# Decay rows kept in SBUF and copied per head into two fixed operand tiles, in a decay attention with two feed-forward layers

## The chip, the cores and the metric

One core of one Trainium2 chip runs the whole program in one launch. The metric is device time in microseconds (us): the median of three runs, and for one execution that was profiled, its own time and the span of its instructions. Engines are called as in the profile: PE is TensorE (matmuls), PEld its weight loads, DVE is VectorE, ACT ScalarE, POOL GpSimd, SP SyncE, which here issues nearly all DMAs in the order of the program.

## What is computed

```
scores = scale * q @ k.T                          # 4 x 8 heads, 576 x 576, head size 64
log_f  = log(clip(f, 1e-4, 1)); cum = cumsum(log_f)
scores = where(causal, -1e9, scores + cum[i] - cum[j])
attn   = softmax(scores);  out = attn @ v
x = out as (2304, 512)
x = (h * relu6(h + 3) / 6) @ w_out,   h = x @ w_in       # 512 -> 2048 -> 512
x = (max(h, 0) + alpha * min(h, 0)) @ w_out2, h = x @ w_in2
```

## The kernel before

The program has two stages: attention, about the first 210 us, and the two feed-forward layers. Attention goes over 16 pairs of heads. A pair is nine units: four blocks of 128 query rows of the even head (positions 0 to 3), one unit that holds the last 64 rows of both heads (position 4, which reads the even head's tiles and then the odd head's, L375 and L377), and four blocks of the odd head (positions 5 to 8). A loop over units writes each engine's work by hand: scores of unit t, maxima of unit t-1, exponentials of t-2, transposes and evictions of t-5; the weights of the feed-forward layers are converted in between by a table of unit numbers (`CONV_ATT`).

The scores of one head take two matmuls that add up in PSUM. Line L363 multiplies `k1` and `q1` (128 rows). Line L364 multiplies `k2` and `q2` (68 rows): rows 0 to 63 hold the low part of q and the high part of k, and rows 64 to 67 carry the decay: the two words of `cum` (high and low) against rows of 1 and of -1. The four tiles of a head come from a pool with three buffers of each.

Where the decay rows come from: in the prologue `cum` of all heads is made in one SBUF tile of 64 partitions, and from it and some constants two DRAM tensors `aq_d` and `ak_d` are written (L502, L504, L523 to L528). For the first two heads `aug_rows` copies the rows from SBUF straight into the tiles (L495 to L498). For each later head h, `prep_head` (at position 3 for the next pair's even head, 7 for its odd head) issues two DMAs that read the four rows of `q2` and of `k2` from DRAM:

```
nc.sync.dma_start(out=q2[64:68].bitcast(F32), in_=aq_d[h % 2, h // 2])
nc.sync.dma_start(out=k2[64:68].bitcast(F32), in_=ak_d[h % 2, h // 2])
```

Then POOL writes `q1` and `k1` (L93). Two units later `prep_low` makes the low parts (POOL L331, DVE L332), and `copy_k` copies the high part of k from `k1` into `k2` by a DMA from SBUF to SBUF (L325; for heads 2 and 3 POOL does it within `prep_head`). `load_head` (L295) reads q and k of a head from DRAM into one of three `rqk` buffers.

SP issues DMAs strictly in this written order, and a DMA that has to wait holds all behind it. In the trace SP issues the copies of a head well ahead of the unit in which they stand, since their buffers are free early.

Of the kernel before, what the change touches and what calls it, by code (L numbers as in the profile page):

```python
# [8 lines left out]
F32 = mybir.dt.float32  # L9
I64 = mybir.dt.int64  # L10
U32 = mybir.dt.uint32
F32R = mybir.dt.float32r
# [9 lines left out]
def decay_attention_ffn2_kernel(ctx, tc, qk, v, f, wi1, wo1, wi2, wo2, alpha, out):  # L22
    nc = tc.nc
# [15 lines left out]
    KT = 5  # L39
# [41 lines left out]
    wo_d = [[dram.tile([128, 2, FT * DM], F32, name=f"wod{ff}{g}") for g in range(NG)] for ff in range(2)]  # L81

    f_d = [dram.tile([128, 4, KH * 256], F32, name=f"fd{g}") for g in range(NC)]
    aq_d = dram.tile([2, 32, 4, QW], F32, name="aq_d")
    ak_d = dram.tile([2, 32, 4, S], F32, name="ak_d")

    def scaled(engine, dst, src, scale=1.0):
        if engine == "A":
# [189 lines left out]
    def attention():  # L278
        with ExitStack() as ax:
# [9 lines left out]
            ps_pv = ax.enter_context(tc.tile_pool(name="ps_pv", bufs=1, space=PSUM))  # L289

            raws, slots, vs, pts, sm, rcs, rcb = {}, {}, {}, {}, {}, {}, {}

            def load_head(h):
                raw = rawp.tile([128, QW + S], F32, tag="raw", name="rqk")
                nc.sync.dma_start(out=raw, in_=qk[h])  # L295
                raws[h] = (raw[:, 0:QW], raw[:, QW:QW + S])
# [3 lines left out]
                nc.sync.dma_start(out=vs[p], in_=v[p // NPAIR, p % NPAIR])  # L300

            def op_tiles(h):
                slots[h] = (opsp.tile([128, QW], F32R, tag="q1", name="q1"),
                            opsp.tile([68, QW], F32R, tag="q2", name="q2"),
                            opsp.tile([128, S], F32R, tag="k1", name="k1"),
                            opsp.tile([68, S], F32R, tag="k2", name="k2"))
                return slots[h]

            def prep_head(h):
                if h not in slots:  # L310
                    q1, q2, k1, k2 = op_tiles(h)
                    nc.sync.dma_start(out=q2[64:68].bitcast(F32), in_=aq_d[h % 2, h // 2])
                    nc.sync.dma_start(out=k2[64:68].bitcast(F32), in_=ak_d[h % 2, h // 2])
                q1, q2, k1, k2 = slots[h]
                rq, rk = raws[h]
                e = AS0[h] if h < 2 else AS
                scaled(e[0], q1, rq, SCALE)
                scaled(e[1], k1, rk)
                if h < 4:
                    scaled(e[2], k2[0:64], rk[0:64])  # L320

            def copy_k(h):
                q1, q2, k1, k2 = slots[h]
                if h >= 4:
                    nc.sync.dma_start(out=k2[0:64].bitcast(F32), in_=k1[0:64].bitcast(F32))  # L325

            def prep_low(h):
                q1, q2, k1, k2 = slots[h]
                rq, rk = raws.pop(h)
                low = nc.vector if h < 2 and LS0[h] == "V" else nc.gpsimd  # L330
                low.tensor_sub(out=k1[64:128], in0=rk[64:128], in1=k1[64:128].bitcast(F32))  # L331
                nc.vector.scalar_tensor_tensor(  # L332
                    out=q2[0:64], in0=rq[0:64], scalar=SCALE, in1=q1[0:64].bitcast(F32),
                    op0=ALU.mult, op1=ALU.subtract)
# [128 lines left out]
                        d.pop(key)  # L463


            NPP = 64
            px = ExitStack()
            pro = px.enter_context(tc.tile_pool(name="pro", bufs=1))
            fl = pro.tile([NPP, S], F32, name="fl")
# [2 lines left out]

            zero = pro.tile([NPP, S], F32, name="zero")
            cum = pro.tile([NPP, S], F32, name="cum")
            aq = pro.tile([NPP, 2, QW], F32, name="aq")
            pro.tile([NPP, 2 * ((KT - 1) * PR + S) - 3 * S - 2 * QW], F32, name="room")
            ak = pro.tile([NPP, 4, S], F32R, name="ak")
            hl = ak[:, 2:4, :]
            nc.gpsimd.memset(zero, 0.0)
            nc.gpsimd.memset(aq, -1.0)  # L480
            for a in range(2):
                nc.gpsimd.memset(aq[32 * a:32 * a + 32, :, 576 - 64 * a:640 - 64 * a], 0.0)

            def aug_consts(a):
                o0 = 576 - 64 * a
                q1, q2, k1, k2 = op_tiles(a)
                (nc.gpsimd if a else nc.vector).memset(k2[64:68].bitcast(F32), 1.0)
                nc.vector.memset(q2[64:68].bitcast(F32), -1.0)
                nc.vector.memset(q2[64:68, o0:o0 + 64].bitcast(F32), 0.0)

            def aug_rows(a):
                r, t0 = slice(32 * a, 32 * a + 1), 512 + 64 * a
                q1, q2, k1, k2 = slots[a]
                w = S if a == 0 else 512
                nc.sync.dma_start(out=q2[64:66, 0:w].bitcast(F32), in_=hl[r, :, 0:w].bitcast(F32))  # L495
                (nc.sync if a else nc.scalar).dma_start(out=k2[66:68].bitcast(F32), in_=hl[r].bitcast(F32))
                if w < S:
                    nc.sync.dma_start(out=q2[64:66, t0:t0 + TAIL].bitcast(F32), in_=hl[r, :, 512:S].bitcast(F32))  # L498

            load_head(1)  # L500
            nc.sync.dma_start(out=alpha_sb, in_=alpha)
            nc.sync.dma_start(out=aq_d.rearrange("a h r c -> (a h) r c")[:, 2:4], in_=aq)  # L502
            for a in range(2):
                nc.sync.dma_start(out=aq_d[a, :, 0:2, 576 - 64 * a:640 - 64 * a],  # L504
                                  in_=zero[32 * a:32 * a + 32, 0:128].rearrange("p (r c) -> p r c", r=2))
            aug_consts(0)
            aug_consts(1)
            make_identity(nc, identb)
            nc.gpsimd.memset(maskb, 0.0)
            nc.gpsimd.affine_select(out=maskb, in_=maskb, pattern=[[-1, 128]], compare_op=ALU.is_ge,  # L510
                                    fill=-1.0e9, base=0, channel_multiplier=1)
            nc.gpsimd.memset(ak[:, 0:2, :].bitcast(F32), 1.0)
            nc.vector.tensor_scalar(out=fl, in0=fl, scalar1=1e-4, scalar2=1.0, op0=ALU.max, op1=ALU.min)
            nc.scalar.activation(out=fl, in_=fl, func=AF.Ln)
            nc.vector.tensor_tensor_scan(out=cum, data0=fl, data1=zero, initial=0.0, op0=ALU.add, op1=ALU.add)
# [2 lines left out]
            nc.vector.tensor_sub(out=hl[:, 1, :], in0=cum, in1=hl[:, 0, :].bitcast(F32))  # L518
            aug_rows(0)
            prep_low(0)  # L520
            aug_rows(1)
            load_head(2)
            nc.sync.dma_start(out=aq_d.rearrange("a h r c -> (a h) r c")[:, 0:2, 0:512], in_=hl[:, :, 0:512].bitcast(F32))  # L523
            for a in range(2):
                ps, t0 = slice(32 * a, 32 * a + 32), 512 + 64 * a
                nc.sync.dma_start(out=aq_d[a, :, 0:2, t0:t0 + TAIL], in_=hl[ps, :, 512:S].bitcast(F32))
            for a in range(2):
                nc.sync.dma_start(out=ak_d[a, 0:NP], in_=ak[32 * a:32 * a + NP].bitcast(F32))  # L528
            load_head(3)
            nc.gpsimd.memset(three, 3.0)  # L530
            make_identity(nc, ident)
# [37 lines left out]
            for t in range(len(units) + max(LV, PB) + 1):  # L569
                now = todo.pop(t, [])  # L570
                for ch in ORD:
                    if ch == "D":
                        for fn in now:
                            fn()
                    if ch == "S" and t < len(units):
                        live[t] = stage1(units[t])
                    for c, lag, fn in (("M", LM, maxes), ("E", LE, exps)):
                        if ch == c and 0 <= t - lag < len(units):
                            live[t - lag] = fn(*live[t - lag])
                    for c, lag, fn in (("T", LT, transposes), ("V", LV, evac)):  # L580
                        if ch == c and 0 <= t - lag < len(units):
                            live[t - lag] = fn(units[t - lag], *live[t - lag])
                if t < len(units):
                    p, ab, i = units[t]
                    pos = t % 9
                    if ab == 1 and i == 3:
                        for d, fn in ((RD, lambda p=p: recips(p)), (SD, lambda p=p: spread(p)),
                                      (PA, lambda p=p: stage3(p, 0)), (PB, lambda p=p: stage3(p, 1))):
                            todo.setdefault(t + d, []).append(fn)
                    if pos == 2:  # L590
                        load_v(p)
                    if pos == QA and 2 * p + 2 < 2 * NP:
                        prep_head(2 * p + 2)
                        todo.setdefault(t + QL, []).append(lambda h=2 * p + 2: prep_low(h))
                        todo.setdefault(t + QL, []).append(lambda h=2 * p + 2: copy_k(h))
                        if p:
                            load_head(2 * p + 3)
                    if pos == QB and 2 * p + 3 < 2 * NP:
                        prep_head(2 * p + 3)
                        todo.setdefault(t + QL, []).append(lambda h=2 * p + 3: prep_low(h))  # L600
                        todo.setdefault(t + QL, []).append(lambda h=2 * p + 3: copy_k(h))
                        if 2 * p + 4 < 2 * NP:
                            load_head(2 * p + 4)
                elif t == len(units) + LE:
                    rx.close()
                    ffn_open()
                for fn in side.pop(t, []):
                    fn()
                for _ in range(DRAIN.get(t, 0)):
                    step()  # L610
# [303 lines left out]
```

## Time and profile before

| | |
|---|---|
| median of 3 runs | 981.56 us (980.86 to 982.42) |
| the profiled execution, its own time | 982.49 us |
| its span, first to last instruction | 980.7 us |
| mean granted clock of TensorE | 0.996 of full speed |
| busy share of the span: PE, DVE, POOL, ACT | 97%, 72%, 61%, 55% |
| chain that ended last: PE, DVE, other | 85%, 8%, 7% |

A busy share is the time in which an engine had an instruction under way. PE is busy nearly all the time, so what counts is the few stretches in which it waits, and how long its instructions take. The chain is followed back from the last instruction to what released each step.

### The profile page before, as it was taken

The page shows a single profiled execution, that of the slowest core. Times are in us where ns is not written, and L with a number is a line of the kernel's source. Part 1 is how long each engine was busy: PE and PEld are TensorE (multiplying, and loading weights), DVE is VectorE, ACT ScalarE, POOL GpSimd, SP SyncE. Part 2 cuts the span into 40 slices and gives each one's busy share as a digit, 9 for nine tenths or more (in the row PEclk, how much of TensorE's full clock was granted, in tenths as well). Part 3 has the DMA queues.
Part 4 walks back from the last instruction along what each step waited for, and adds up shares of the span by engine and source line. Part 5 has one row for each costly group of instructions (what it writes and reads, how often), then busy time and mean ns, then how long its engine had stood idle before and what let it go on. Part 6 is the DMA issues. An engine that isn't in the chain of part 4 may idle for free.

```text
span 980.7 us, 15789 instructions
## 1 busy us (share of the span) xinstructions
PE 955.6 (97%) x5488; PEld 860.4 (88%) x5488; DVE 705.7 (72%) x1274; ACT 539.7 (55%) x1348; POOL 594.4 (61%) x583
## 2 busy tenths in 40 slices
PE   5999999999999999999999999999999999999998
PEld 4767766678999999999999999899898988898897
DVE  7898979956697777876788666347897778625454
ACT  5678877777555554555564456644454546343231
POOL 7567589956646665578476379565646668422231
PEclk9999999999999999999999999999999999999999
DMA  7646576501414443410468732413434410253541
GB/s 211 201 136 213 181 250 196 144 35 43 161 65 182 183 183 108 160 59 9 166 246 312 272 130 108 161 65 140 173 118 182 182 65 17 103 204 139 216 161 64
DMA packets 36195, 145.79 MB, mean 149 GB/s; under 512 B 4860, under 2 KB 4860, under 8 KB 33012
## 3 DMA queue, kind: packets, MB, share of 16 engines
q1 hardware_dynamic: 36112, 144.79, 42.0%
q8 instruction: 43, 0.70, 0.3%
q14 instruction: 36, 0.29, 0.1%
q10 hardware_dynamic: 4, 0.00, 0.0%
HBM read 97.21 MB, written 43.42 MB: 143 GB/s over the span
## 4 chain that ended last, share of the span: by engine, by line
PE 85%; DVE 8%; issue 2%; POOL 2%; ACT 1%; SPq 1%; DMA 1%; POOLq 0%; DVEq 0%; ACTq 0%
PE o L744 20%; PE hA L704 20%; PE o L742 19%; PE hC L704 10%; PE hB L704 5%; PE pv L453 4%; DVE nm L340 2%; PE tp L396 2%; PE sc L363 2%; DVE q L332 1%; PE sc L364 1%; DVE pt L407 1%; POOL g L687 1%; DMA k<-ak_d 1%; PE sc L375 0%
## 5 line engine op out<-in xcount | busy, mean ns | idle before, releaser
L687 POOL TENSOR_TENSOR g<-t,g 128x384 fp32r<-128x384 f32 x192 | 205.6, 1071 | 287.6 <-ACT g L686 270.4
L742 PE MATMUL o<-g,wo 128*128 128x384 f32 x1152 | 232.2, 340 | 1.8 <-POOL wo L187 1.1
L704 PE MATMUL hA<-xh,wi 128*128 128x384 f32 x768 | 224.3, 338 | 1.1 <-DVE hD L718 0.7
L744 PE MATMUL o<-wo,g 128*128 128x512 f32 x864 | 223.2, 394 | 0.0
L742 PEld LDWEIGHTS o<-g,wo 128*128 128x128 f32 x1152 | 205.0, 189 | 3.2 <-POOL wo L187 1.4
L686 ACT CAST g<-t 128x384 fp32r<-128x384 f32 x192 | 98.6, 514 | 176.8 <-DVE t L681 91.8
L744 PEld LDWEIGHTS o<-wo,g 128*128 128x128 f32 x864 | 160.6, 188 | 25.8
L762 DVE TENSOR_TENSOR r<-o,r 128x512 f32<-128x512 f32 x126 | 86.7, 688 | 86.2 <-PE o L744 85.7
L704 PEld LDWEIGHTS hA<-xh,wi 128*128 128x128 f32 x768 | 141.5, 188 | 4.7 <-DVE hD L718 1.0
L704 PE MATMUL hA<-xl,wi 128*128 128x384 f32 x384 | 129.5, 337 | 0.0
L751 DVE SCALAR_TENSOR_TENSOR r<-o,r 128x384 f32<-128x384 f32 x168 | 92.1, 552 | 49.1 <-PE o L742 48.3
L704 PE MATMUL hC<-xh,wi 128*128 128x384 f32 x384 | 114.4, 338 | 0.0
L348 ACT ACTIVATE p<-sc,nm 128x128 f32<-128x128 f32 (+4 forms) x160 | 84.2, 530 | 16.6 <-DVE nm L340 14.5
L340 DVE TENSOR_REDUCE nm<-sc 128x1 f32<-128x128 f32 (+4 forms) x160 | 71.6, 469 | 6.1 <-PE sc L365 4.0
L704 PEld LDWEIGHTS hA<-xl,wi 128*128 128x128 f32 x384 | 72.1, 188 | 3.2
L704 PEld LDWEIGHTS hC<-xh,wi 128*128 128x128 f32 x384 | 71.3, 189 | 2.1 <-issue 0.2
L248 POOL TENSOR_TENSOR xl<-r,xh 128x384 fp32r<-128x384 f32 x59 | 69.7, 1197 | 3.3 <-ACT xh L243 2.8
L396 PE MATMUL tp<-ident,p 128*128 128x128 f32 x384 | 68.6, 282 | 1.0 <-ACT pt L412 0.6
L363 PE MATMUL sc<-k,q 128*128 128x256 f32 (+2 forms) x128 | 55.0, 429 | 12.2 <-DVE k L331 8.8
L709 ACT COPY s<-hA 128x384 f32<-128x384 f32 x96 | 45.8, 477 | 35.1 <-PE hA L704 34.9
L704 PE MATMUL hC<-xl,wi 128*128 128x384 f32 x192 | 65.0, 338 | 0.0
L704 PE MATMUL hB<-xh,wi 128*128 128x384 f32 x192 | 57.1, 338 | 0.0
(133 smaller groups left out, 1725.6 us busy)
## 6 DMA issues: line engine op xcount, KB each, us to landing
wid<-wi SPq DMA_DIRECT2D x24, 896.0 KB
wi<-wid SPq DMA_DIRECT2D x12, 1792.0 KB
rqk<-in_qk SPq DMA_DIRECT2D x32, 608.0 KB
raw<-in_wi SPq DMA_DIRECT2D x32, 512.0 KB
raw<-in_wo SPq DMA_DIRECT2D x32, 512.0 KB
wod<-wo SPq DMA_DIRECT2D x24, 512.0 KB
wo<-wod SPq DMA_DIRECT2D x12, 1024.0 KB
vt<-in_v SPq DMA_DIRECT2D x16, 320.0 KB
```

Of the source, the lines that this page charges most:

```text
L248: e.tensor_sub(out=XS[k][1][:, b, c], in0=x, in1=XS[k][0][:, b, c].bitcast(F32))
L340: nc.vector.tensor_reduce(out=nm[:, i:i + 1], in_=src, axis=AX.X, op=ALU.max, negate=True)
L348: nc.scalar.activation(out=pt[:, c0:c0 + cw], in_=src, func=AF.Exp, bias=nm[:, 0:1], scale=1.0, accum_out=dsts[i])
L363: nc.tensor.matmul(out=sc[:, 0:n], lhsT=q1[:, qs], rhs=k1[:, 0:n], start=True, stop=False)
L396: nc.tensor.transpose(tp[:, j, :], pt[:, 128 * j:128 * j + 128], ident)
L686: nc.scalar.copy(out=gt[n][i][:, 0], in_=hold["g"])
L687: nc.gpsimd.tensor_sub(out=gt[n][i][:, 1], in0=hold["g"], in1=gt[n][i][:, 0].bitcast(F32))
L704: nc.tensor.matmul(out=h, lhsT=a, rhs=b[:, x, kc], start=new and kc + e == 0, stop=kc == KH - 1 and e == 2, skip_group_check=not new)
L742: nc.tensor.matmul(out=o[:, 0:NB], lhsT=a[:, cs], rhs=b, start=st, stop=sp)
L744: nc.tensor.matmul(out=o, lhsT=b[:, cs], rhs=a, start=st, stop=sp)
L751: later(0, lambda: nc.vector.scalar_tensor_tensor(out=acc, in0=o[:, 0:NB], scalar=1.0 / 6.0, in1=acc, op0=ALU.mult, op1=ALU.add))
L762: nc.vector.tensor_add(out=acc, in0=o, in1=acc)
```

## The change

The two DRAM tensors and the eight DMAs that fill them go, with the POOL memsets behind them. The tile of `cum` words, now called `hl`, stays in SBUF through the whole attention stage. `q2` and `k2` are no longer taken from the pool of three: there is one fixed pair of tiles for all even heads (`lowq[0]`, `lowk[0]`) and one for all odd heads (`lowq[1]`, `lowk[1]`), so the constant rows are written once. For every head `aug_rows` now copies the two rows of `cum` into `q2` and into `k2` from SBUF: two DMAs for an even head, three for an odd one. These are issued in `copy_k`, which stands two units later than `prep_head` (position 5 for the even head, position 0 of the next pair for the odd head) and now ahead of `prep_low`. For heads 2 and 3 the POOL copy of k's high part moves from `prep_head` to there. In the prologue the loads of heads 2 and 3 stand further ahead.

```diff
-    aq_d = dram.tile([2, 32, 4, QW], F32, name="aq_d")
-    ak_d = dram.tile([2, 32, 4, S], F32, name="ak_d")
...
+            lowq = [lowp.tile([68, QW], F32R, name=f"q2{a}") for a in range(2)]
+            lowk = [lowp.tile([68, S], F32R, name=f"k2{a}") for a in range(2)]
+            hl = lowp.tile([NPP, 2, S], F32R, name="hl")
...
-                slots[h] = (opsp.tile([128, QW], F32R, tag="q1", name="q1"),
-                            opsp.tile([68, QW], F32R, tag="q2", name="q2"),
-                            opsp.tile([128, S], F32R, tag="k1", name="k1"),
-                            opsp.tile([68, S], F32R, tag="k2", name="k2"))
+                slots[h] = (opsp.tile([128, QW], F32R, tag="q1", name="q1"), lowq[h % 2],
+                            opsp.tile([128, S], F32R, tag="k1", name="k1"), lowk[h % 2])
...
             def prep_head(h):
-                if h not in slots:
-                    q1, q2, k1, k2 = op_tiles(h)
-                    nc.sync.dma_start(out=q2[64:68].bitcast(F32), in_=aq_d[h % 2, h // 2])
-                    nc.sync.dma_start(out=k2[64:68].bitcast(F32), in_=ak_d[h % 2, h // 2])
-                q1, q2, k1, k2 = slots[h]
+                q1, q2, k1, k2 = op_tiles(h)
...
-                if h < 4:
+                if h < 2:
                     scaled(e[2], k2[0:64], rk[0:64])
...
             def copy_k(h):
                 q1, q2, k1, k2 = slots[h]
+                aug_rows(h)
                 if h >= 4:
                     nc.sync.dma_start(out=k2[0:64].bitcast(F32), in_=k1[0:64].bitcast(F32))
+                else:
+                    scaled("P", k2[0:64], raws[h][1][0:64])
...
-            def aug_rows(a):
-                r, t0 = slice(32 * a, 32 * a + 1), 512 + 64 * a
-                q1, q2, k1, k2 = slots[a]
+            def aug_rows(h):
+                a = h % 2
+                row, t0 = 32 * a + h // 2, 512 + 64 * a
+                r = slice(row, row + 1)
+                q2, k2 = lowq[a], lowk[a]
                 w = S if a == 0 else 512
                 nc.sync.dma_start(out=q2[64:66, 0:w].bitcast(F32), in_=hl[r, :, 0:w].bitcast(F32))
-                (nc.sync if a else nc.scalar).dma_start(out=k2[66:68].bitcast(F32), in_=hl[r].bitcast(F32))
+                (nc.sync if h else nc.scalar).dma_start(out=k2[66:68].bitcast(F32), in_=hl[r].bitcast(F32))
                 if w < S:
                     nc.sync.dma_start(out=q2[64:66, t0:t0 + TAIL].bitcast(F32), in_=hl[r, :, 512:S].bitcast(F32))
...
             aug_rows(0)
             prep_low(0)
+            load_head(2)
             aug_rows(1)
-            load_head(2)
-            nc.sync.dma_start(out=aq_d.rearrange("a h r c -> (a h) r c")[:, 0:2, 0:512], in_=hl[:, :, 0:512].bitcast(F32))
...
             load_head(3)
...
-                        todo.setdefault(t + QL, []).append(lambda h=2 * p + 3: prep_low(h))
                         todo.setdefault(t + QL, []).append(lambda h=2 * p + 3: copy_k(h))
+                        todo.setdefault(t + QL, []).append(lambda h=2 * p + 3: prep_low(h))
```

How SP's queue changes is seen at two places. The first is the prologue, from the copies of the first heads' decay rows on (`rqk` is the load of a head, `ak` or `hl` the tile of `cum` words). Before:

```order
L495 DMA q2_172<-ak_160 2x1x576
L495 DMA q2_179<-ak_160 2x1x512
L496 DMA k2_181<-ak_160 2x1x576
L498 DMA q2_179<-ak_160 2x1x64
L295 DMA rqk_209<-in_qk 128x1216
L523 DMA aq_d_118<-ak_160 64x2x512
L526 DMA aq_d_118<-ak_160 32x2x64 x2
L528 DMA ak_d_119<-ak_160 16x2304 x2
L295 DMA rqk_216<-in_qk 128x1216
L300 DMA vt_262<-in_v 128x640
L312 DMA q2_273<-aq_d_118 4x640
L313 DMA k2_275<-ak_d_119 4x576
```

and now:

```order
L489 DMA q20_150<-hl_154 2x1x576
L298 DMA rqk_196<-in_qk 128x1216
L489 DMA q21_151<-hl_154 2x1x512
L490 DMA k21_153<-hl_154 2x1x576
L492 DMA q21_151<-hl_154 2x1x64
L298 DMA rqk_201<-in_qk 128x1216
L303 DMA vt_249<-in_v 128x640
L489 DMA q20_150<-hl_154 2x1x576
L490 DMA k20_152<-hl_154 2x1x576
```

The load of head 2 moves ahead of three copies, the writes to DRAM are gone, and head 2's rows come from `hl`.

The second place is the turn from the tenth to the eleventh pair, about 130 us into the span, where the converted weights are stored to DRAM (`wid`); `raw` is a fetch of weights, `vt` of v. Before:

```order
L325 DMA k2_2147<-k1_2146 64x576
L192 DMA wid00_83<-wi_1001 128x1792
L300 DMA vt_2239<-in_v 128x640
L312 DMA q2_2255<-aq_d_118 4x640
L313 DMA k2_2257<-ak_d_119 4x576
L295 DMA rqk_2262<-in_qk 128x1216
L192 DMA wid00_83<-wi_1001 128x1792
L118 DMA raw_2265<-in_wi1 128x512
L325 DMA k2_2257<-k1_2256 64x576
```

and now:

```order
L489 DMA q21_151<-hl_154 2x1x512
L490 DMA k21_153<-hl_154 2x1x576
L492 DMA q21_151<-hl_154 2x1x64
L323 DMA k21_153<-k1_2103 64x576
L190 DMA wid00_83<-wi_976 128x1792
L303 DMA vt_2196<-in_v 128x640
L298 DMA rqk_2215<-in_qk 128x1216
L190 DMA wid00_83<-wi_976 128x1792
L116 DMA raw_2218<-in_wi1 128x512
L489 DMA q20_150<-hl_154 2x1x576
L490 DMA k20_152<-hl_154 2x1x576
L323 DMA k20_152<-k1_2212 64x576
```

The copies of the odd head (21) now write the one pair of odd tiles, and stand with all that follows behind them; the copies of the even head (22) follow the stores as the copy of `k2` did.

## Rows read from the trace of the kernel before

**Rows 1.** The busy time of each engine by stretch, with clock, DMA share, GB/s.

```profile
core 0: us, PE busy (x) PEld busy (x) DVE busy (x) ACT busy (x) POOL busy (x), PEclk, DMA share, GB/s
31.00:55.00 24.00, 23.49 (x183) 16.92 (x182) 21.50 (x44) 18.35 (x67) 12.79 (x13) 1.00 0.56 177
245.00:600.00 355.00, 354.90 (x2019) 354.50 (x2019) 270.92 (x478) 187.42 (x379) 225.57 (x211) 1.00 0.43 156
```

**Rows 2.** The chain that ended last, in order of time, 8 to 80 us.

```profile
17.19 4.98 DMA k<-ak_d
```

**Rows 3.** PE's timeline: start, us, line, idle time before.

```profile
19.24 0.36 PE L363 MATMUL sc<-k,q 128*128 128x256 f32 x1
22.30 0.35 PE L364 MATMUL sc<-k,q 68*128 68x256 f32 x1 [2.70 <-DMA k<-ak_d]
...
27.49 0.29 PE L377 MATMUL sc<-k,q 68*128 68x288 f32 x1
...
35.19 0.28 PE L364 MATMUL sc<-k,q 68*128 68x256 f32 x1
...
38.96 0.30 PE L377 MATMUL sc<-k,q 68*128 68x288 f32 x1
```

**Rows 4.** POOL's timeline, the low part of head 2's k.

```profile
17.51 1.41 POOL L331 TENSOR_TENSOR k<-rqk,k 64x576 fp32r<-64x576 f32 x1
```

**Rows 5.** Stretches after that wait, columns as in rows 1.

```profile
23.90:27.20 3.30, 3.30 (x16) 2.78 (x15) 2.90 (x7) 2.35 (x8) 2.86 (x4) 0.50 0.87 318
27.30:30.60 3.30, 3.30 (x31) 2.65 (x30) 2.97 (x7) 2.38 (x9) 3.13 (x4) 1.00 0.46 97
```

**Rows 6.** PE's timeline: two ends of odd heads, and the units that follow.

```profile
34.21 0.40 PE L364 MATMUL sc<-k,q 68*128 68x512 f32 x1
...
38.43 0.29 PE L377 MATMUL sc<-k,q 68*128 68x288 f32 x1
...
194.16 0.39 PE L364 MATMUL sc<-k,q 68*128 68x512 f32 x1
...
199.02 0.30 PE L377 MATMUL sc<-k,q 68*128 68x288 f32 x1
```

**Rows 7.** SP's timeline: copies within SBUF, start and time of the issue.

```profile
9.96 0.56 SPq L498 DMA_DIRECT2D q<-ak  x1
10.56 0.40 SPq L295 DMA_DIRECT2D rqk<-in_qk  x1
...
112.66 0.47 SPq L325 DMA_DIRECT2D k<-k  x1
```

**Rows 8.** Short stretches after the copy at 112.66, columns as in rows 1.

```profile
114.60:114.80 0.20, 0.20 (x3) 0.03 (x3) 0.20 (x2) 0.20 (x2) 0.20 (x1) 1.00 0.15 46
114.80:115.00 0.20, 0.20 (x4) 0.20 (x4) 0.20 (x3) 0.20 (x1) 0.20 (x1) 1.00 0.00 0
```

**Rows 9.** SP's timeline at the turn to the eleventh pair.

```profile
129.26 0.47 SPq L325 DMA_DIRECT2D k<-k  x1
129.82 0.55 SPq L192 DMA_DIRECT2D wid<-wi  x1
...
136.45 0.47 SPq L325 DMA_DIRECT2D k<-k  x1
```

**Rows 10.** A stretch behind these issues, columns as in rows 1.

```profile
136.00:138.00 2.00, 2.00 (x21) 1.60 (x20) 1.97 (x4) 1.89 (x7) 1.84 (x3) 1.00 1.04 396
```

**Rows 11.** Timeline of PE and its weight loads, 128 to 146 us.

```profile
130.44 0.40 PE L364 MATMUL sc<-k,q 68*128 68x512 f32 x1
...
131.19 0.19 PEld L363 LDWEIGHTS sc<-k,q 128*128 128x128 f32 x1
...
131.30 0.19 PEld L364 LDWEIGHTS sc<-k,q 68*128 68x128 f32 x1
```

**Rows 12.** The same one pair later.

```profile
143.82 0.19 PEld L363 LDWEIGHTS sc<-k,q 128*128 128x128 f32 x1
...
144.02 0.19 PEld L364 LDWEIGHTS sc<-k,q 68*128 68x128 f32 x1
...
146.42 0.50 PE L363 MATMUL sc<-k,q 128*128 128x512 f32 x1 [0.40 <-ACT p L348]
```

More of the change, by code (lines that the diff above doesn't have):

```diff
@@ L291, in attention @@
             raws, slots, vs, pts, sm, rcs, rcb = {}, {}, {}, {}, {}, {}, {}
+            lowp = rx.enter_context(tc.tile_pool(name="lowp", bufs=1, side="right"))
+            lowq = [lowp.tile([68, QW], F32R, name=f"q2{a}") for a in range(2)]
+            lowk = [lowp.tile([68, S], F32R, name=f"k2{a}") for a in range(2)]
+            NPP = 64
+            hl = lowp.tile([NPP, 2, S], F32R, name="hl")
             def load_head(h):
@@ L463, in stage3 @@
                         d.pop(key)
-            NPP = 64
             px = ExitStack()
@@ L474, in attention @@
             cum = pro.tile([NPP, S], F32, name="cum")
[L475 to L478, printed above, removed]
             nc.gpsimd.memset(zero, 0.0)
-            nc.gpsimd.memset(aq, -1.0)
-            for a in range(2):
-                nc.gpsimd.memset(aq[32 * a:32 * a + 32, :, 576 - 64 * a:640 - 64 * a], 0.0)
             def aug_consts(a):
                 o0 = 576 - 64 * a
-                q1, q2, k1, k2 = op_tiles(a)
+                q2, k2 = lowq[a], lowk[a]
                 (nc.gpsimd if a else nc.vector).memset(k2[64:68].bitcast(F32), 1.0)
@@ L489, in aug_consts @@
                 nc.vector.memset(q2[64:68, o0:o0 + 64].bitcast(F32), 0.0)
-            def aug_rows(a):
-                r, t0 = slice(32 * a, 32 * a + 1), 512 + 64 * a
-                q1, q2, k1, k2 = slots[a]
+            def aug_rows(h):
+                a = h % 2
+                row, t0 = 32 * a + h // 2, 512 + 64 * a
+                r = slice(row, row + 1)
+                q2, k2 = lowq[a], lowk[a]
                 w = S if a == 0 else 512
                 nc.sync.dma_start(out=q2[64:66, 0:w].bitcast(F32), in_=hl[r, :, 0:w].bitcast(F32))
-                (nc.sync if a else nc.scalar).dma_start(out=k2[66:68].bitcast(F32), in_=hl[r].bitcast(F32))
+                (nc.sync if h else nc.scalar).dma_start(out=k2[66:68].bitcast(F32), in_=hl[r].bitcast(F32))
                 if w < S:
@@ L501, in attention @@
             nc.sync.dma_start(out=alpha_sb, in_=alpha)
[L502 to L505, printed above, removed]
             aug_consts(0)
@@ L511, in attention @@
                                     fill=-1.0e9, base=0, channel_multiplier=1)
-            nc.gpsimd.memset(ak[:, 0:2, :].bitcast(F32), 1.0)
             nc.vector.tensor_scalar(out=fl, in0=fl, scalar1=1e-4, scalar2=1.0, op0=ALU.max, op1=ALU.min)
@@ L520, in attention @@
             prep_low(0)
+            load_head(2)
             aug_rows(1)
-            load_head(2)
-            nc.sync.dma_start(out=aq_d.rearrange("a h r c -> (a h) r c")[:, 0:2, 0:512], in_=hl[:, :, 0:512].bitcast(F32))
[L524 to L528, printed above, removed]
             load_head(3)
@@ L593, in attention @@
                         prep_head(2 * p + 2)
+                        todo.setdefault(t + QL, []).append(lambda h=2 * p + 2: copy_k(h))
                         todo.setdefault(t + QL, []).append(lambda h=2 * p + 2: prep_low(h))
-                        todo.setdefault(t + QL, []).append(lambda h=2 * p + 2: copy_k(h))
                         if p:
@@ L599, in attention @@
                         prep_head(2 * p + 3)
+                        todo.setdefault(t + QL, []).append(lambda h=2 * p + 3: copy_k(h))
                         todo.setdefault(t + QL, []).append(lambda h=2 * p + 3: prep_low(h))
-                        todo.setdefault(t + QL, []).append(lambda h=2 * p + 3: copy_k(h))
                         if 2 * p + 4 < 2 * NP:
```

## The prediction

> **What bounds the kernel now.** I read the table of stretches first, to see which engine each stage hangs on. In the feed-forward part PE is busy 354.90 of 355.00 us, and the change touches nothing there; in a stretch of attention PE is still busy 23.49 of 24.00 us and DVE 21.50 [rows 1]. So a microsecond that PE gains or loses in attention goes through to the end, and a price laid on any other engine counts only where PE then waits. The next view is the chain of waits, which tells what PE waits for. Its longest piece in the first 80 us is a transfer: the read of head 2's decay rows of `k2` from `ak_d`, 4.98 us from its issue at 17.19 [rows 2]. PE's timeline shows the price: the first matmul of `k1` and `q1` of head 2 starts at 19.24, the one of `k2` and `q2` only at 22.30, after 2.70 us of idle time that this transfer ended [rows 3]. The reader should see that this read goes through DRAM, so it stands behind the write that fills `ak_d`, and that no later head pays it.
>
> **What the change gives back.** (a) The wait of 2.70 us. Head 2's rows now come from SBUF as soon as PE has read head 0's tiles for the last time, four units earlier, and its load stands ahead of three copies of about 0.60 us each, so it starts about 2 us sooner than 10.56 [rows 7]. What is late next there is the low part of head 2's k on POOL; it ended at 18.92 even before [rows 4], ahead of 19.24. So all of the wait goes: 2.7 us. (b) The clock. From 23.9 to 27.2, after the wait, the granted clock stood at 0.50 of full speed, the 1.2 GHz level, and at 1.00 (2.4 GHz) behind it [rows 5]. The same matmuls, from the even head's first L364 to the last L377 of the pair, took 27.49 - 22.30 = 5.19 us in that pair and 38.96 - 35.19 = 3.77 us in the next [rows 3]. Without the wait I take this fall to be gone: 1.4 us. Bounds: 0 and 1.4. The DRAM writes, the POOL memsets and the reads of `aq_d` free queues on which nothing ended late, and I cost them at nothing.
>
> **What it costs at every odd head.** Before, a head had a buffer of `q2` and `k2` to itself while the head ahead of it was read, and SP could issue its copies early: the copy of `k2` of an odd head went out at 129.26, while PE read the last of the odd head before it at 130.44 [rows 9, 11]. Now there is one pair of odd tiles. Its copies wait until PE has ended the odd head's last L364, at position 8, and the next odd head is first read at position 4 of the next pair (the second L377). That time is 38.43 - (34.21 + 0.40) = 3.82 us at the first such place with a head from 4 on, and 199.02 - (194.16 + 0.39) = 4.47 us at the last of 14 [rows 6]. Into it must go three issues of rows, one of the `k2` copy, and its transfer. A small copy within SBUF took SP 0.60 us from one issue to the next (9.96 to 10.56) [rows 7]. The copy of `k2` issued at 112.66 had its last packets between 114.6 and 114.8, 2.1 us later [rows 7, 8]; the landing and PE's start add an estimated 0.2 to 0.3. Together 3 x 0.60 + 2.1 + 0.25 = 4.15 us, so 0.3 us late where the time is 3.82. An even head has two row copies and a longer time, some 7.4 us (27.49 + 0.29 to 35.19) [rows 3], so those are hidden.
>
> The Trainium skill, DMA: Bandwidth & Descriptors, section Rules for kernel authors, speaks against this part: issue a DMA early, compute, and wait late, because the fixed setup then overlaps. The change issues it late. By the section Anatomy of one DMA (2.0 us and bytes over 436 GB/s) the copy of 64 x 576 words would be an estimated 2.3 us, and the sum 4.1; the trace's 2.1 us and landing agree with that.
>
> A lateness of 0.3 us counts where PE itself is the chain at that point. Where DVE is, the maxima of these units are not yet due. I take three places, 1.0 us. Bounds: 0 where an issue takes 0.40 as the load's did at 10.56 [rows 7] (3 x 0.40 + 2.35 = 3.55), and 14 x 0.35 = 4.9 us if every place pays.
>
> **What it costs once, at the weight stores.** SP's order is fixed, so whatever stands behind the odd copies waits with them. At the turn to the eleventh pair that is the store of converted weights (`wid`), then vt, a load, the second store and a fetch, and behind these the copies of head 22. Before, the store went out at 129.82 [rows 9]. Now it stands behind head 21's copies, which wait for PE's L364 to end at 130.44 + 0.40 [rows 11]: 130.84 + 3 x 0.60 + 0.56 = 133.2, 3.4 us later. These transfers fill the DMA engines: their share is 1.04 at 136 to 138 us [rows 10]. So nothing makes up for a late start. And the last of them is only just in time: head 22's copy, issued at 136.45 [rows 9], is read by the first L364 of the next pair, whose weight load starts 0.20 us after that of L363 (143.82, 144.02) [rows 12], where one pair earlier it was 0.11 (131.19, 131.30) [rows 11]. I read these 0.09 us as a wait for the landing, 7.5 us after the issue instead of 2.3. With the queue 3.4 us later, PE waits 3.4 us. A wait of 0.40 us for ACT three units on [rows 12] is then covered; I take 0.5, and 2.9 us remain. Behind it everything is as late as PE. Bounds: 0, if the order in the queues is not what holds that copy, and 4.0, where each issue takes 0.8 us, a third more than in the row.
>
> The Trainium skill, DMA: Bandwidth & Descriptors, section Queues, rings and completion order, says that a DMA engine takes descriptors of one ring in their order. By that rule head 22's copy can't pass the stores, and the 2.9 us stand; the 7.5 us read from the trace agree.
>
> (c) After this wait, which is longer than the one at 19.6, I expect the clock at 0.50 once more, with the price of (b): 1.4 us. Bounds 0 and 1.7, half of the 3.3 us that the stretch at 0.50 has in the row.
>
> **Sum.** -2.7 - 1.4 + 1.0 + 2.9 + 1.4 = +1.2 us. The profiled execution took 982.49, 0.93 above the median of the runs, so it would be 983.7 and the median 982.8 us.
>
> **Rivals.** I call 0.2% (2.0 us) the least that a measurement of this kernel tells from no change: 979.6 to 983.5.
> - *All but the clock.* The wait at 144 is split or shorter, and the clock holds: 981.4. For it: waits of 0.4 us in attention [rows 12] left the clock full. Against: 2.70 us did not.
> - *The stores' delay is hidden.* If head 22's copy is not held by the queue, or there is slack behind PE there, only (a), (b) and the odd heads are left: -4.1 + 1.0, 978.5, faster. For it: the 0.09 us on which I read the landing are small, and a share over 1 is a mean over engines. Against: the copies before it fill the engines.
> - *Every odd head is late* (slower). A row copy that reads one partition may take SP longer than those of the prologue, or land behind a load. With a supposed 0.7 us for each issue a copy is 0.6 us late where the time is 3.82, 9 us over 14 places, less where the time is longer or DVE is the chain; with 5 us in place of 1.0 the time is 986.8. It decides once the odd heads cost 1.7 us in all (983.5), 0.12 us at each place. For it: PE is busy 98% of attention [rows 1], so there is little slack to take it up. Against: the later places have over 4.4 us [rows 6].
>
> **How the numbers follow.** All terms as in the sum 0.42; no second fall of the clock 0.20; stores hidden 0.22; every odd head late 0.16. Of the first case, centred at 982.8, I put 0.28 within 0.2%, 0.13 above and 0.01 below; the second lies within for 0.17, with 0.02 below and 0.01 above; of the third 0.20 are faster; the fourth is slower. Together faster 0.23, same 0.47, slower 0.30. The range has to hold the third case and most of the fourth: 978.0 to 986.4. The likeliest case alone: 981.0 to 984.6.
>
> **What would show it.** Right: PE goes from L363 to L364 of head 2 without a wait near 19.4, and the clock stays at 1.00 from 23.9 to past 100 us; SP's three row copies of an odd head start right behind the end of an L364, about 0.6 us apart; PE has short waits at L377 that DMAs of `k2` end; one wait of about 3 us at the first L364 of the twelfth pair, and a stretch at 0.50 behind it. Wrong: row copies issued in 0.3 us, which takes the odd term away; no wait near 140 us, which makes it 978.5; or idle time in L377 at most pairs, which makes it slower.

## The result

The changed kernel took 987.58 us (median of 4 runs, 985.48 to 988.02), the kernel before 981.47 beside it: a ratio of 1.0055, 95% interval 1.0039 to 1.0071. It is slower by 6.1 us at the medians, and lies above the range of the prediction (978.0 to 986.4). The two profiled executions differ by 5.5 us of span (986.2 and 980.7).

The gain and the costs that the prediction named are all there; the sizes differ. PE's timeline of the changed kernel has the first `L364` of a pair, an odd head's last `L364` and the next odd head's second `L377` (start, us, line, idle time before), in answer to [rows 3, 6, 12]:

```profile
19.59 0.37 PE L363 MATMUL sc<-k,q 128*128 128x256 f32 x1
19.79 0.28 PE L364 MATMUL sc<-k,q 68*128 68x256 f32 x1
...
31.21 0.40 PE L364 MATMUL sc<-k,q 68*128 68x512 f32 x1
...
32.19 0.28 PE L364 MATMUL sc<-k,q 68*128 68x256 f32 x1
...
36.08 0.37 PE L377 MATMUL sc<-k,q 68*128 68x288 f32 x1 [0.50 <-DMA k<-k]
...
132.72 0.28 PE L364 MATMUL sc<-k,q 68*128 68x256 f32 x1
...
148.90 0.55 PE L364 MATMUL sc<-k,q 68*128 68x256 f32 x1 [3.03 <-DMA k<-k]
...
162.62 0.28 PE L364 MATMUL sc<-k,q 68*128 68x256 f32 x1
...
200.44 0.28 PE L364 MATMUL sc<-k,q 68*128 68x256 f32 x1
```

Head 2's `L364` follows its `L363` without a wait (19.59, 19.79). The third pair starts at 32.19 in place of 35.19, 3.0 us sooner. From there the gain drains away: the eleventh pair starts at 132.72 where it was at 131.42 before, and the wait at the twelfth pair is 3.03 us. From the end of an odd head's last `L364` to the next odd head, 31.21 + 0.40 to 36.08, are 4.47 us, against 3.82 before [rows 6]. At 13 of the 14 places the time is now 4.41 to 5.03 us (9.27 at the turn); before, it was 3.82 to 4.17 us at the first eight and 4.18 to 5.03 at the last six.

The chain of waits of the changed kernel says what fills it (start, us, what):

```profile
32.28 0.57 SPq L490
...
32.90 0.56 SPq L492
...
33.56 2.38 DMA k<-k
35.95 0.14 issue
...
139.83 8.93 DMA k<-k
```

The three row copies and then the copy of `k2` go out one behind the other, the last 1.95 us after the tile came free at 31.61; it is under way for 2.38. The row at 139.83 is head 22's copy behind the two stores, 8.93 us. SP's timeline shows the place (start, issue time), in answer to [rows 7, 9]:

```profile
133.43 0.56 SPq L492 DMA_DIRECT2D q<-hl  x1
134.09 0.52 SPq L323 DMA_DIRECT2D k<-k  x1
134.71 0.53 SPq L190 DMA_DIRECT2D wid<-wi  x1
...
136.86 1.04 SPq L190 DMA_DIRECT2D wid<-wi  x1
...
139.83 0.52 SPq L323 DMA_DIRECT2D k<-k  x1
```

The table of stretches answers to [rows 1, 5]: PE is busy 22.31 of 24 us where it was 23.49, and the clock stands at 0.50 behind the wait at 148.90.

```profile
31.00:55.00 24.00, 22.31 (x170) 16.21 (x172) 21.72 (x47) 17.97 (x65) 12.36 (x14) 1.00 0.58 180
147.40:154.10 6.70, 5.20 (x23) 4.21 (x24) 2.60 (x10) 3.15 (x11) 4.01 (x6) 0.50 0.78 213
154.20:157.60 3.40, 3.40 (x31) 2.75 (x30) 3.21 (x7) 2.65 (x9) 3.32 (x3) 1.00 0.81 309
```

For all kernels of this study I read the same five rows, the first `L364` of the first, third, eleventh, thirteenth and sixteenth pair, and took differences. This table shows where a kernel gains and loses, in us; the second stretch is eight pairs long. Each row is one profiled execution. In the second stretch the four kernels with the tiles of before have 96.20 to 96.23, and the three with the copies and loads of the changed kernel 100.05 to 100.53, so there a difference of less than half a microsecond says nothing. A ratio is taken to the kernel before in runs on the same chip, whose medians were 981.47 to 982.16.

| kernel | median, us | ratio to before, 95% | pairs 1-2 | pairs 3-10 | pairs 11-12 | pairs 13-15 |
|---|---|---|---|---|---|---|
| before | 981.47 | | 25.20 | 96.23 | 24.71 | 39.00 |
| changed | 987.58 | 1.0055 (1.0039-1.0071) | 22.12 | 100.53 | 29.90 | 37.82 |
| k2 first | 984.02 | 1.0022 (1.0013-1.0032) | 21.90 | 98.37 | 28.16 | 38.23 |
| stores early | 985.26 | 1.0033 (1.0022-1.0044) | 21.83 | 100.10 | 25.06 | 39.34 |
| loads early | 986.68 | 1.0047 (1.0034-1.0061) | 22.13 | 99.65 | 29.14 | 37.79 |
| k2 first, stores early | 981.23 | 0.9993 (0.9984-1.0002) | 22.26 | 98.50 | 24.72 | 39.37 |
| all three edits | 979.18 | 0.9976 (0.9966-0.9985) | 22.16 | 96.21 | 24.77 | 38.94 |
| all three, heads 2 and 3 by DMA | 979.02 | 0.9963 (0.9950-0.9976) | 21.59 | 96.24 | 25.23 | 38.48 |
| changed, heads 2 and 3 by DMA | 987.75 | 1.0058 (1.0045-1.0070) | 21.57 | 100.05 | 30.09 | 37.75 |
| before, stores late | 982.50 | 0.9998 (0.9987-1.0008) | 24.09 | 96.22 | 24.76 | 38.94 |
| before, third head ahead | 983.59 | 1.0022 (1.0014-1.0031) | 25.64 | 96.20 | 24.77 | 38.92 |
| before, third head behind | 981.23 | 0.9990 (0.9980-0.9999) | 24.07 | 96.22 | 24.76 | 38.96 |

The changed kernel gains 3.1 us in the first stretch, loses 4.3 in the second and 5.2 in the third, and wins 1.2 back in the last.

### The profile page after: what moved, and what is told of

Read it like the earlier page. It is cut to its first block, busy times and chain, and to the rows that moved or that the text cites. A ratio compares the mean times of both kernels' runs of the same rounds, so it can differ in the third digit from the quotient of the medians.

```text
span 986.2 us, 15776 instructions
## 1 busy us (share of the span) xinstructions
PE 956.5 (97%) x5488; PEld 859.6 (87%) x5488; DVE 706.4 (72%) x1274; ACT 540.9 (55%) x1348; POOL 589.1 (60%) x579
## 4 chain that ended last, share of the span: by engine, by line
PE 85%; DVE 6%; issue 3%; POOL 2%; DMA 2%; ACT 1%; SPq 0%; ACTq 0%; POOLq 0%; DVEq 0%
PE o L727 20%; PE hA L687 19%; PE o L725 19%; PE hC L687 10%; PE hB L687 5%; PE pv L453 4%; PE tp L396 2%; DMA k<-k 2%; PE sc L363 2%; DVE nm L340 2%; PE sc L364 1%; PE sc L377 1%; DVE q L332 1%; POOL g L670 1%; PE tr L435 1%
## 5 line engine op out<-in xcount | busy, mean ns | idle before, releaser
L363 PE MATMUL sc<-k,q 128*128 128x256 f32 (+2 forms) x128 | 55.4, 433 | 12.4 <-DVE k L331 8.7
L701 DVE TENSOR_TENSOR hC<-hC,s 128x384 f32<-128x384 f32 x48 | 27.1, 564 | 42.0 <-PE hC L687 38.9
```

The lines of the kernel that those rows point to most:

```text
L363: nc.tensor.matmul(out=sc[:, 0:n], lhsT=q1[:, qs], rhs=k1[:, 0:n], start=True, stop=False)
```

## The experiments

The theory after the result: the third stretch is lost by the stores behind the waiting copies, and the second by the copies of `k2` that come fourth. The rival for the second is that VectorE sets the spacing, since some waits of `L377` are put down to it.

**The k2 copy first.**

```diff
             def copy_k(h):
                 q1, q2, k1, k2 = slots[h]
-                aug_rows(h)
                 if h >= 4:
                     nc.sync.dma_start(out=k2[0:64].bitcast(F32), in_=k1[0:64].bitcast(F32))
                 else:
                     scaled("P", k2[0:64], raws[h][1][0:64])
+                aug_rows(h)
```

> Against the changed kernel only the order of the copies of one head is turned: its 64 rows k2 from k1 go ahead of the decay rows, for heads 2 and 3 the GpSimd copy too. Theory: the odd heads lose time because their k2 copy is issued fourth, 0.03 + 3 x 0.64 us after the tile is free, and lands 4.35 to 4.5 us after it, against 3.82 to about 4.1 that the pair leaves; in first place it lands about 2.4 us after it, and the last of the short row copies (issued 2.0 us after it, 1.7 us under way) at about 3.7. The 4.3 us between the second and the eleventh pair come back: 983 to 984 us, and the spacing from the end of the last L364 to the second head's L377 falls from 4.41 to 5.03 us to about 3.9. The wait at the twelfth pair stays. Rival: that spacing is set by VectorE (the waits of L377 that are put down to nm and pt), so the order of the copies changes nothing: 987.5.

Measured 984.02. The spacing fell to 3.82 to 4.13 us at its first five places, as before the change, and the second stretch by 2.16 us (100.53 to 98.37), half of what it had lost. The rival falls as the whole cause; but the theory is not the whole either.

**The stores one unit earlier.**

```diff
-... wi0 90 wi1 93 wo0 99 wo1 102 ...
+... wi0 89 wi1 92 wo0 98 wo1 101 ...
```

> Against the changed kernel the four stores of the weights (wi0, wi1, wo0, wo1) are issued one unit earlier, so that the first stands ahead of the odd head's waiting copies, as it did before the change. Theory: the 3.0 us wait at the first L364 of the twelfth pair and the half clock of 6.8 us behind it go (3.55 + 1.64 us), of which up to 1.2 was won back in later pairs anyway: 982.5 to 983.7 us, no granted clock of 0.5 between 18 and 980 us. The odd heads stay late. Rival: the two stores' bytes reach the queues before the next even head's copy in any order, so its landing stays near 8.9 us: 987.5.

Measured 985.26. The third stretch came from 29.90 to 25.06, by 4.84 us, and the clock stays at 1.00 to the end of attention; the last stretch, which had won 1.2 back, is 39.34 again. So the profiled execution is only 3.2 us shorter (988.02, 984.84) and the median 2.3; 982.5 to 983.7 were expected. PE's wait at the twelfth pair is 0.16 us in place of 3.03, and the clock is full behind it. First PE's timeline, then the stretch:

```profile
144.84 0.36 PE L364 MATMUL sc<-k,q 68*128 68x256 f32 x1 [0.16 <-DMA k<-k]
```

```profile
132.00:200.00 68.00, 63.69 (x479) 44.83 (x478) 60.69 (x126) 53.45 (x194) 59.52 (x57) 1.00 0.59 187
```

In the changed kernel the wait and the half clock come from the stores' place.

**Both.** 

> Both edits together: the k2 copy ahead of the decay rows and the stores one unit earlier. Theory: the two losses are separate and add up; what is left is the gain of 3.0 us at the second and third pair: 978 to 979.5 us, faster than both kernels. Rival: the time of a pair in this stretch is set by VectorE as well, so that what one edit gives is lost again at the next wait: 982 to 984.

Measured 981.23, by neither expectation, and not told from the kernel before (0.9984 to 1.0002). The third stretch is as before, the second still 2.27 us too long, and the excess lies in single pairs: the ninth took 13.58 us where it was 12.34. VectorE's and GpSimd's timelines of this kernel there:

```profile
105.22 0.81 DVE L332 SCALAR_TENSOR_TENSOR q<-rqk,q 64x640 fp32r<-64x640 f32 x1
105.95 1.90 DVE L147 SCALAR_TENSOR_TENSOR wc<-raw,wc 128x512 uint32<-128x512 uint32 x1
```

```profile
105.32 1.99 POOL L331 TENSOR_TENSOR k<-rqk,k 64x576 fp32r<-64x576 f32 x1
```

In the kernel before, the same conversion (line 149 there) took 0.68 us. GpSimd did nothing beside it, since that head's `L331` had run in the pair before:

```profile
107.75 0.68 DVE L149 SCALAR_TENSOR_TENSOR wc<-raw,wc 128x512 uint32<-128x512 uint32 x1
```

```profile
103.45 1.47 POOL L331 TENSOR_TENSOR k<-rqk,k 64x576 fp32r<-64x576 f32 x1
```

Why GpSimd is later stands in this kernel's rows of GpSimd and of SP: GpSimd waited 3.71 us for the odd head's load, and SP issued that load at 96.17, 3.25 us after the pair's start at 92.92.

```profile
103.70 0.73 POOL L91 TENSOR_SCALAR q<-rqk 128x640 fp32r<-128x640 f32 x1 [3.71 <-DMA rqk<-in_qk]
```

```profile
96.17 0.38 SPq L298 DMA_DIRECT2D rqk<-in_qk  x1
```

GpSimd could begin only 7.5 us after that issue (103.70); a fetch of weights and one of v had gone out just ahead of the load, at 95.25 and 95.64. In the kernel before the same load went out 0.59 us after the pair's start (96.02, 95.43), and GpSimd began that head at 101.54 without a wait.

```profile
96.02 0.36 SPq L295 DMA_DIRECT2D rqk<-in_qk  x1
```

So the rest of the loss, by these rows, is the loads that stand behind the waiting copies.

**The loads ahead of the copies.** Each load takes the slot of the one before it.

```diff
                     if pos == 2:
                         load_v(p)
+                    if pos == 3 and 2 * p + 4 < 2 * NP:
+                        load_head(2 * p + 4)
+                    if pos == 6 and 2 * p + 5 < 2 * NP:
+                        load_head(2 * p + 5)
...
-                        if p:
-                            load_head(2 * p + 3)
...
-                        if 2 * p + 4 < 2 * NP:
-                            load_head(2 * p + 4)
```

> Against the changed kernel each load of a head's q and k (L298) is issued half a pair sooner: it stands in the queue where the load of the head before it stood, ahead of the copies that wait for TensorE. Theory: in the changed kernel the odd head's load is issued 3.1 us after the pair's start in place of 1.65, GpSimd prepares the head up to 3 us later, and its L331 falls beside VectorE's conversion at the next pair's start, which then takes 1.90 us in place of 0.68; the ninth pair runs 13.45 us in place of 12.34. With the loads ahead of the copies GpSimd's L331 of the odd head starts by 9.5 us into its pair again: the ninth pair 1.0 us shorter, 986.5 us. The late k2 copies and the stores stay. Rival: GpSimd waits for something else than the load (its operand tiles), and nothing changes: 987.5.

Measured 986.68. That can't be told from the changed kernel by the time alone (1.0034 to 1.0061 against 1.0039 to 1.0071). In the trace the second stretch is 0.88 us shorter, and the ninth pair 12.93 in place of 13.45, half of what was expected of it. The mechanism is there: `L331` of the odd head now starts 3.6 us sooner (102.53, 106.12) and no longer runs beside VectorE's conversion. One thing in the expectation is off: in the changed kernel the conversion that is stretched there is `L143`, 1.51 us in place of 0.42; the 1.90 us of `L147` belong to the kernel with the first two edits. GpSimd's and VectorE's timelines of the changed kernel:

```profile
106.12 1.41 POOL L331 TENSOR_TENSOR k<-rqk,k 64x576 fp32r<-64x576 f32 x1
```

```profile
106.31 1.51 DVE L143 TENSOR_SCALAR wc<-wc 128x512 uint32<-128x512 uint32 x1
```

and with the loads early:

```profile
102.53 1.41 POOL L331 TENSOR_TENSOR k<-rqk,k 64x576 fp32r<-64x576 f32 x1
```

```profile
106.03 0.42 DVE L143 TENSOR_SCALAR wc<-wc 128x512 uint32<-128x512 uint32 x1
```

That the late copies, which stayed, cover the other half is my reading; the next run fits it.

**All three edits.** 

> The k2 copy first, the stores one unit earlier and the loads half a pair sooner, together. Theory: against the kernel with the first two alone the eighth and ninth pair come down from 12.15 and 13.58 us to 11.5 and 12.4, so the gain of the second and third pair is kept to the end: 979 to 979.5 us. Rival: what these pairs lose there is made by where VectorE's and GpSimd's work falls, which shifts by chance when anything is moved, and is lost at other places: 981.

Measured 979.18 us, faster than both kernels (0.9966 to 0.9985 of the kernel before). The second stretch is 96.21 against 96.23 before, the third 24.77 against 24.71: nothing is given back. PE's timeline at the second, third, eleventh and thirteenth pair:

```profile
20.96 0.28 PE L364 MATMUL sc<-k,q 68*128 68x256 f32 x1
...
32.39 0.28 PE L364 MATMUL sc<-k,q 68*128 68x256 f32 x1
...
128.60 0.28 PE L364 MATMUL sc<-k,q 68*128 68x256 f32 x1
...
153.37 0.28 PE L364 MATMUL sc<-k,q 68*128 68x256 f32 x1
```

The three edits change only when SP issues a transfer; the shared tiles are as in the changed kernel. So the shared tiles alone cost nothing here: with the same tiles and another order in SP's queue all of the loss is gone.

**Heads 2 and 3 with k2 by DMA,** on the changed kernel and on the three edits (`if h >= 4` becomes `if h >= 2`).

> Against the changed kernel heads 2 and 3 take their k2 by the copy from k1 through SyncE's queue, as the later heads do, in place of GpSimd's scaled copy. Theory: the second pair runs 12.40 us instead of less because VectorE's L332 for the fourth head took 2.07 us beside GpSimd's L331, and the GpSimd copy pushed both later; without it GpSimd ends 0.7 us sooner and L332 falls to about 1.3: the second pair 0.5 us shorter, 987.0 us. Rival: head 2's k2 then lands behind its rows at about 18.6 us and head 3's at about 23.5 us, later than they are wanted (19.79 and 23.44), and the pair starts later: 988 to 989.

> The three edits together, and heads 2 and 3 with their k2 by the copy from k1 through SyncE's queue as well, so that GpSimd has 0.7 us less to do per head at the second pair. Theory: head 3's L331 on GpSimd is done before VectorE's L332 starts, neither is stretched (2.04 us and 2.07 us seen), and the second pair begins as soon as the first ends: 978.5 to 979 us. Rival: head 3's k2 copy, in front of its row copies, waits in SyncE's queue for GpSimd's k1, and the rows land later than wanted: 979.5 to 980.

Measured 987.75 and 979.02. The first stretch is 0.55 and 0.57 us shorter, and the end does not show it: neither can be told from the kernel without the edit.

**The stores late in the kernel before** (`wi0 90 wi1 93` becomes `wi0 93 wi1 94`).

> The kernel before, with only the two stores wid at the turn to the eleventh pair issued later: the first behind the load that stood 3.3 us after it in the queue. Theory: the wait at the first L364 of the twelfth pair and the half clock behind it come from the stores' place alone and need no shared tiles; the copy of the even head (issued at about 136.5) stands behind 1.8 MB again and lands about 2 to 3 us after it is wanted at 144.05, the granted clock falls to 0.5 behind it: 984 to 986 us. Rival: it needs the copies held up by TensorE as well, since here the copy is issued 3.4 us sooner than in the changed kernel (139.83); then nothing changes: 981.5.

Measured 982.50, no change: the rival holds. The stores moved in the queue, but with copies that wait for no reader SP was there early, as its timeline shows:

```profile
130.79 0.38 SPq L192 DMA_DIRECT2D wid<-wi  x1
...
131.69 1.34 SPq L192 DMA_DIRECT2D wid<-wi  x1
...
135.22 0.47 SPq L325 DMA_DIRECT2D k<-k  x1
```

The first store went out 1.0 us later than before, the second 1.8 us sooner (131.69, 133.48), head 22's copy 1.2 us sooner (135.22, 136.45), and PE's wait at the twelfth pair was 0.16 us:

```profile
143.16 0.36 PE L364 MATMUL sc<-k,q 68*128 68x256 f32 x1 [0.16 <-DMA rqk<-in_qk]
```

So the late place in the program's order cost nothing in a queue that nothing holds; stores that really go out 3 us late in this kernel were not tried.

**The third head alone, in the kernel before,** with its rows copied from SBUF into tiles of its own.

```diff
+            aug_consts(0, 2)
...
             aug_rows(1, 1)
             load_head(2)
+            aug_rows(0, 2)
             nc.sync.dma_start(out=aq_d.rearrange("a h r c -> (a h) r c")[:, 0:2, 0:512], in_=hl[:, :, 0:512].bitcast(F32))
...
             load_head(3)
```

> Against the kernel before, only the third head's decay rows come from SBUF by the copies that the first two heads have, into its own operand tiles with constants written for them; all other heads read theirs from DRAM as before, and no tile is shared by two heads at a time. Theory: the gain of the change is the third head's rows alone (a PE wait of 2.7 us), and the losses all come from the shared tiles: second pair from 19.8 us in place of 22.3, no clock of 0.5 at 24 us, and nothing is given back: 978.5 to 979 us. Rival: the fourth head's rows, still from DRAM, end last next, or the VectorE work of the second pair, so that less than 1 us stays: 981.

Measured 983.59, slower, by neither expectation: the constants and copies stood in front of the first pair (which began at 10.80 in place of 9.99) and of the fourth head's data, so the second pair took 15.36 us. Part of that is the clock, which stood at 0.50 behind waits of 1.1 and 0.7 us close together:

```profile
28.00:29.00 1.00, 1.00 (x7) 0.99 (x6) 0.97 (x3) 0.81 (x3) 0.92 (x3) 0.50 0.27 98
```

With the copies behind `load_head(3)` and the constants behind the first `prep_low`:

> The kernel before with the third head's decay rows from SBUF into its own tiles again, but their copies issued behind the DRAM writes and the fourth head's load, and the constants written by VectorE after the first head's L332 instead of ahead of everything. Theory: in the earlier run the copies and memsets stood in front of what the first, second and fourth head needed (the first pair began 0.8 us later, the fourth head's load was issued at 16.22 us, the second pair took 15.36 us); moved behind them, the 2.7 us of the third head are gained without that: second pair from about 20 us, 978.5 to 979.5 us. Rival: the fourth head still reads from DRAM, its L312 and L313 wait for the writes until about 19 us, and the second pair is stretched by what the start gained: 981 to 982.

Measured 981.23 (0.9980 to 0.9999). The rival's time came. The first stretch is 24.07; the second pair takes 13.05 us, and PE waits there 0.73 us for the fourth head's `L331` on GpSimd. The load of that head still stands behind the DRAM writes: it is issued at 14.55, against 10.98 in the changed kernel, and GpSimd begins the head at 21.15, against 17.35. By these rows the gain needs both heads' data without the DRAM writes ahead of them, as the change has it. That GpSimd waits there for the load is not shown; the trace names PE's `L400`.

## Why the prediction was wrong

The step that failed is the odd heads: "I take three places, 1.0 us". It measured 4.30 us over the second stretch, for two reasons. Alone, the `k2` copy first gives back 2.16 us and the loads early 0.88; together, with the stores early, they give back 4.32 (100.53 to 96.21).

- *The places.* The estimate of one copy was near: 4.15 us, against 4.47 at 36.08 (0.03 + 3 x 0.64 + 2.38 + 0.14). (The 2.3 us that the prediction takes from the Trainium skill, DMA: Bandwidth & Descriptors, section Anatomy of one DMA, are there a fit to DMAs that GpSimd issues; SP's copy was under way for 2.38.) What was wrong is that VectorE would cover most of it. The prediction read two of the 14 places, 3.82 and 4.47; all eight places of the second stretch had 3.82 to 4.17 us. Their times grew by 5.8 us in sum, and 4.30 of these, half a microsecond a pair, came through. The rival "every odd head is late" had this, with 986.8, and I gave it 0.16. "PE is busy 98% of attention" stood beside it and should have decided.
- *The loads.* "Whatever stands behind the odd copies waits with them" was costed at the stores alone. The head loads stand there at every pair; they made GpSimd late, and its `L331` fell on VectorE's conversion. With the `k2` copy first and the stores early this was 2.3 us (98.50 to 96.21), in the changed kernel 0.9 (100.53 to 99.65).

The stores and (c) were right in mechanism and a little small: the eleventh pair, which ends with the wait, took 16.18 us in place of 12.63 (3.55, predicted 2.9), the twelfth 13.72 in place of 12.08 (1.64, predicted 1.4). "Behind it everything is as late as PE" was not: 1.2 us came back in the last pairs. Only the four kernels with the long wait at the twelfth pair have less than 38.3 us there, the others 38.48 to 39.37; so the wait is made good in part, by what was not tried. The rival of a hidden delay falls with the 3.03 us.

The gain: (a) was right, the wait is gone. With (b) 4.1 us were predicted and 3.1 came. The first pair came down from 12.31 to 9.72 us, by 2.6; the second from 12.89 to 12.40 only, though the clock was full. There the chain runs through VectorE, whose `L332` took 2.07 us beside GpSimd (below). In three other kernels (stores early, loads early, all three edits) `L332` took 0.81 and the second pair 11.43 to 11.44 us, but the first pair took 10.39 to 10.73, and the whole stretch, 21.83 to 22.16, is hardly shorter than 22.12. In that first pair PE was busy all the time, and its matmuls kept the longer times of the program's start until later. PE's timeline, in the changed kernel and with all three edits, has the same matmul (the granted clock reads 1.00 at both):

```profile
17.88 0.33 PE L364 MATMUL sc<-k,q 68*128 68x384 f32 x1
```

```profile
18.23 0.52 PE L364 MATMUL sc<-k,q 68*128 68x384 f32 x1
```

Why they did is open. And (b) is not there in every execution: in the kernel with late stores, whose first pairs are those of before, PE waited 2.15 us at the same place and the clock stayed full; its first stretch took 24.09, not 25.20. Against that one the changed kernel gains 2.0 us, not 3.1. Its rows of PE's timeline and of the table of stretches, in answer to [rows 3, 5]:

```profile
22.41 0.36 PE L364 MATMUL sc<-k,q 68*128 68x256 f32 x1 [2.15 <-DMA k<-ak_d]
```

```profile
23.90:27.20 3.30, 3.30 (x27) 2.69 (x26) 3.12 (x9) 2.38 (x9) 2.86 (x4) 1.00 0.85 326
```

With the measured sizes the sum closes: -3.1 + 4.3 + 5.2 - 1.2 = +5.2 of the 5.5 us of span.

## What to carry to other kernels

A copy into a shared tile that waits for its reader also holds everything behind it in its queue: cost every transfer in that queue at every round, not the conspicuous one. Put the copy that takes longest first among those that wait, and loads that wait for nothing ahead of them; here that turned a loss of 6.1 us into a gain of 2.3. Where PE is busy 98%, cost a lateness at every place until a row shows what covers it.

## What was not expected of the hardware

**VectorE and GpSimd take turns.** In the changed kernel `L331` on GpSimd starts at 20.04 and takes its usual 1.41 us; `L332` on VectorE starts 0.02 us later and takes 2.07. With all three edits `L332` starts first, 0.05 us ahead, takes 0.81, and `L331` takes 2.04. First the two timelines of the changed kernel, then those of the kernel with all three edits:

```profile
20.06 2.07 DVE L332 SCALAR_TENSOR_TENSOR q<-rqk,q 64x640 fp32r<-64x640 f32 x1
```

```profile
20.04 1.41 POOL L331 TENSOR_TENSOR k<-rqk,k 64x576 fp32r<-64x576 f32 x1
```

```profile
21.16 0.81 DVE L332 SCALAR_TENSOR_TENSOR q<-rqk,q 64x640 fp32r<-64x640 f32 x1
```

```profile
21.21 2.04 POOL L331 TENSOR_TENSOR k<-rqk,k 64x576 fp32r<-64x576 f32 x1
```

Whoever comes second takes nearly the rest of the other's time and its own (1.39 + 0.81 against 2.07, 0.76 + 1.41 against 2.04). Above, at 105 us, this goes through three instructions: `L331` behind `L332`, `L147` behind `L331`. The Trainium skill, SBUF — State Buffer, section SBUF: two separate sides, says this: the two engines' shared port pair is an exclusive lock for a whole instruction, not a share. The traces agree. In these two executions the starts are hundredths of a microsecond apart, and the second pair is 1.0 us shorter where VectorE is first (12.40, 11.43); but the first pair is as much longer there (9.72, 10.73), so that the turn by itself gains time is not shown.

**The clock after a wait.** Behind 2.15 us of waiting PE's clock stayed at 1.00 in one execution. Behind 2.70 it fell to 0.50 in another [rows 3, 5], and behind 1.1 and 0.7 us close together in a third (the third head ahead). Behind 2.48 us, in the kernel with the `k2` copy first, it fell as well. Behind 3.03 it read 0.50 for 6.7 us, in 5.2 of which PE was busy. What decides it was not tried. PE's timeline of the kernel with the `k2` copy first:

```profile
145.59 0.36 PE L364 MATMUL sc<-k,q 68*128 68x256 f32 x1 [2.48 <-DMA k<-hl]
```

**SP's issue of a copy within SBUF** takes 0.56 to 0.58 us for two short rows and 0.52 for `k2`, more than the 0.36 to 0.38 of the loads of 128 rows from DRAM shown above; three of them hold the queue for 1.9 us (3 x 0.64).
